# Feature projections as pairs of 64-row matmuls, with a mode-aware list schedule and a new step order

## The chip, the cores and the metric

One core of a Trainium2 chip. The metric is the device time of one execution in microseconds (us), lower is better. Most kernels here were run four times. Ratios are computed as the mean time of one kernel's runs over that of the kernel before in the same rounds, so they are not quite the ratio of the medians that are quoted.

## The reference

Linear attention with an exponential feature map, then a mixture of experts in which every token visits all eight experts. Only the first part is touched by the change.

```python
batch, n_heads, seq, head_dim, d_feat = 8, 8, 576, 64, 128
def phi(x):
    proj = np.einsum('bhsd,df->bhsf', x, w_phi)          # contraction over 64
    proj = proj - np.max(np.abs(proj), axis=-1, keepdims=True)
    return np.concatenate([np.exp(proj), np.exp(-proj)], axis=-1)
q_p, k_p = phi(q), phi(k)
kv  = np.einsum('bhsf,bhsd->bhfd', k_p, v)
num = np.einsum('bhsf,bhfd->bhsd', q_p, kv)              # den: the same with sums of k_p
# ... x = num/den; routing P by 8 Sinkhorn iterations
# out = sum over e of P[:, e] * (relu(x @ w1[e]) @ w2[e])
```

The contraction of the projection is 64 long, and TensorE has 128 rows. Two heads (a "pair") are stacked on the 128 partitions, so there are two ways to project them: one matmul against a weight that is zero in the half of the other head, or two matmuls of 64 rows each, one per head, in the two row halves of the array at once.

## The kernel before

All operations of the kernel are first put into a plan with an assumed duration and its dependences, then a list scheduler sorts them: it keeps a clock per engine and always issues the operation that can start first, ties going to the step order, a string of 322 letters. The sorted list is then the fixed program of each engine. Nothing is moved at run time. An engine that has to wait waits with everything behind it.

```python
wphi2 = a_in.tile([128, 2, DF], BF16)      # [64 rows of w_phi | 0] and [0 | 64 rows of w_phi]

def tokens(pp, stat, n, r, takes=()):      # scores of 128 tokens, both heads in one matmul
    for c in range(n):                     # n = 4
        pe(256, lambda c=c: mm(pp[1][2 * c // n]()[:, 1024 // n * c % 512:][:, 0:256],
                               stat(c), wphi2f, True, True), ...)

def feature_rows(pt, mov, r):              # query features, transposed
    for x in range(2):
        pe(512, lambda x=x: mm(pt[1][x]()[:, 0:512], wphi2[:, x, :], mov(), True, True), ...)
```

From the third batch on, q and k are loaded by a transfer that GpSimd issues, into one of two `qk` buffers. A transposing transfer issued by SyncE then turns the buffer into `qkT`, after which the buffer may be loaded again. GpSimd also computes: the negated maxima and the scaled v of every pair.

```python
def load_qk(b, hh, nh, t, r=()):           # b >= 2; "POOL" is GpSimd's queue
    for x, src in ((1, k), (0, q)):
        dma("POOL", nh << 17, 230, lambda x=x, src=src: nc.gpsimd.dma_start(out=t["qk"]()...))
def turn_qk(t):
    dma("SP", 1 << 19, 148, lambda: nc.sync.dma_start_transpose(out=t["T"]()..., in_=t["qk"]()...))
...
pool(8, lambda: nc.gpsimd.tensor_scalar_mul(m()[:, 1], m()[:, 2], -1.0), ...)     # in pair_a
exp(16, lambda: em(), lambda: m()[:, 1:3], 1.0, ...)                              # ScalarE needs it
pool(1024, lambda: nc.gpsimd.tensor_tensor(out=s["v"]()..., op=ALU.mult), ...)
```

The softmax here doesn't subtract the row's maximum and nothing guards it: scores larger than these inputs give would overflow.

## Time and profile before

| | before |
|---|---|
| median | 1026.8 us (1026.7 to 1027.5, 4 runs) |
| attention, to the last gate matmul | 0 to 205.6 us |
| the rest, same work in both kernels | 821 us |

The prediction shows the page's head, the table by stage and the groups concerned. In such a table each row is a stretch of time, and "busy" is the time in which an engine has an instruction open. A matmul's record holds a tail of 164 ns beyond its pace, so gaps shorter than that can't be seen in TensorE's busy time.

### The profile page before, as it was taken

How to read it: one execution, taken by the hardware profiler on the slowest of the kernel's cores; microseconds unless marked ns; L12 is line 12 of the kernel's file. 1: busy time of each engine (PE TensorE's matmuls, PEld its weight loads, DVE VectorE, ACT ScalarE, POOL GpSimd, SP SyncE). 2: the span in 40 equal slices, each digit the busy share in tenths (PEclk: the TensorE clock that was granted, in tenths of full speed). 3: DMA queues.
4: the chain of work that ended last, by engine and by line, in shares of the span. 5: the costliest groups of instructions: out<-in, count | busy, mean ns of one | idle time of the engine just before them, and what ended most of it. 6: DMA issues, size and time to landing. Idle time of an engine off the chain costs nothing.

```text
span 1026.8 us, 24281 instructions
## 1 busy us (share of the span) xinstructions
PE 1008.1 (98%) x9469; PEld 837.9 (82%) x9504; DVE 823.5 (80%) x1600; ACT 703.9 (69%) x1530; POOL 458.5 (45%) x480
## 2 busy tenths in 40 slices
PE   7899999999999999999999999999999999999998
PEld 4666666645888888888888888888888888888886
DVE  7999989987888887787777877787778877787775
ACT  7999999834888766666666666666665666666663
POOL 5768664400334444444444434544444433444342
PEclk9999999999999999999999999999999999999999
DMA  9999978170232611161115211341116111614333
GB/s 235 192 197 179 177 137 130 37 154 19 85 104 85 124 42 42 47 129 43 48 46 112 54 43 42 75 102 42 42 46 131 42 42 43 130 36 125 133 124 124
DMA packets 112501, 96.03 MB, mean 94 GB/s; under 512 B 54145, under 2 KB 87041, under 8 KB 112385
## 3 DMA queue, kind: packets, MB, share of 16 engines
q1 hardware_dynamic: 80576, 70.55, 26.5%
q0 software_dynamic: 31648, 23.86, 16.6%
q8 instruction: 74, 1.21, 0.5%
q14 instruction: 43, 0.34, 0.1%
q10 hardware_dynamic: 160, 0.07, 0.0%
HBM read 94.98 MB, written 14.16 MB: 106 GB/s over the span
## 4 chain that ended last, share of the span: by engine, by line
PE 93%; ACT 2%; DVE 1%; DMA 1%; SPq 1%; issue 1%; POOL 0%; DVEq 0%; ACTq 0%
PE ps L1273 74%; PE ps L573 17%; PE ps L856 2%; DMA acc<-in_q_dram 1%; ACT q L569 1%; ACT k L569 0%; SPq L495 0%; ACT wx L569 0%; SPq L551 0%; PE ps L885 0%; DMA xd<-S 0%; DVE ps L864 0%; DVE hT L1305 0%; DVE m L565 0%; POOL wx L761 0%
## 5 line engine op out<-in xcount | busy, mean ns | idle before, releaser
L1428 POOL TENSOR_TENSOR acc<-acc,V 128x512 f32<-128x512 f32 x248 | 314.8, 1280 | 484.5 <-ACT V L1425 426.7
L1301 ACT COPY U<-ps 128x512 f32<-128x512 f32 x378 | 217.0, 586 | 166.2 <-PE ps L1273 150.9
L1305 DVE CUSTOM_DVE_ANT_0 hT<-ps,U 128x512 bf16<-128x512 f32 x378 | 254.6, 687 | 87.7 <-PE ps L1273 59.9
L1425 ACT ACTIVATE V<-ps,P 128x256 f32<-128x256 f32 x496 | 208.1, 473 | 90.7 <-PE ps L1273 82.1
L1413 DVE SCALAR_TENSOR_TENSOR acc<-ps,P,acc 128x256 f32<-128x256 f32 x372 | 159.1, 478 | 69.5 <-PE ps L1273 69.2
L1273 PEld LDWEIGHTS <-S 128*128 128x128 bf16 x1984 | 194.1, 98 | 22.6 <-issue 0.2
L1273 PEld LDWEIGHTS <-T 128*128 128x128 bf16 x1512 | 148.0, 98 | 17.2
L1273 PEld LDWEIGHTS <-hT 128*128 128x128 bf16 x1488 | 145.6, 98 | 16.8
L1273 PE MATMUL ps<-X,T 128*128 128x256 bf16 x1008 | 152.4, 273 | 0.0
L1273 PE MATMUL ps<-T,S 128*128 128x256 bf16 x1056 | 135.8, 273 | 0.0
L1273 PEld LDWEIGHTS <-wx 128*128 128x128 bf16 x1152 | 112.7, 98 | 13.6 <-issue 0.2
L1181 DVE TENSOR_TENSOR S<-hT 128x1024 bf16<-128x1024 bf16 x124 | 87.2, 712 | 10.1 <-ACT hT L1310 9.9
L1273 PEld LDWEIGHTS <-w 128*128 128x128 bf16 x864 | 84.5, 98 | 9.8
L1273 PE MATMUL ps<-xT,wx 128*128 128x256 bf16 x576 | 88.4, 273 | 0.1
L1273 PE MATMUL ps<-X,wx 128*128 128x256 bf16 x576 | 86.8, 273 | 0.0
L1310 ACT ACTIVATE hT<-ps 128x512 bf16<-128x512 f32 x126 | 73.2, 606 | 9.8 <-PE ps L1273 9.8
L1273 PE MATMUL ps<-wx,hT 128*128 128x256 bf16 x560 | 77.6, 273 | 0.0
L1273 PE MATMUL ps<-xT,T 128*128 128x256 bf16 x504 | 76.7, 273 | 0.0
L573 PE MATMUL ps<-xT,w 128*128 128x512 bf16 x270 | 70.5, 379 | 0.7
L573 PE MATMUL ps<-w,hT 128*128 128x512 bf16 x276 | 69.8, 379 | 0.7 <-ACT q L569 0.2
L1273 PE MATMUL ps<-T,hT 128*128 128x256 bf16 x496 | 69.2, 273 | 0.0
L1273 PE MATMUL ps<-xT,w 128*128 128x256 bf16 x432 | 66.5, 273 | 0.0
(129 smaller groups left out, 1426.5 us busy)
## 6 DMA issues: line engine op xcount, KB each, us to landing
X<-xd SPq DMA_DIRECT2D x126, 256.0 KB, 2.7
wx<-in_moe_w_dram POOLq DMA_DIRECT2D x8, 1024.0 KB, 12.4
v_m<-in_v_dram SPq DMA_DIRECT2D x15, 512.0 KB, 5.6
out_dram<-acc SPq DMA_DIRECT2D x14, 512.0 KB, 2.9
w<-in_moe_w_dram POOLq DMA_DIRECT2D x6, 1024.0 KB, 12.1
xd<-S SPq DMA_DIRECT2D x18, 256.0 KB, 2.1
qk<-in_k_dram POOLq DMA_DIRECT2D x12, 256.0 KB, 5.5
qk<-in_q_dram POOLq DMA_DIRECT2D x12, 256.0 KB, 6.4
```

Source lines behind the costliest of these rows:

```text
L569: act(el, lambda: nc.scalar.activation(out=dst(), in_=src(), func=ACT.Exp, bias=0.0, scale=scale), r, w)
L573: nc.tensor.matmul(out_, lhsT=lhsT, rhs=rhs, start=start, stop=stop)
L856: pe(65, lambda j=j: nc.tensor.matmul(pn()[:, j * D1:j * D1 + D1], lhsT=s["T"][x]()[:, j % 2, 2 * h + j // 2, :] if j < 4 else r["T"][x]() ...
L1181: lambda: f.tensor_tensor(out=out_(), in0=x(), in1=y(), op=op), r, w, **kw)
L1273: pe(256, lambda i=i, k=k, z=z: nc.tensor.matmul(bank()[:, 256 * i:256 * i + 256], lhsT=lhs(k, i), rhs=rhs(k), start=first and z, stop=k = ...
L1301: act(512, lambda: nc.scalar.copy(out=u[fp][n]().rearrange("p a b -> p (a b)"), in_=x[fp]()), [x[fp]], [u[fp][n]])
L1305: dve(515, lambda: nc.vector._custom_dve(ADD_SAT, out=out_(fp, i, j), in0=bank[fp]().rearrange("p (a b) -> p a b", a=2), in1=u[fp][n](), s ...
L1310: act(512, lambda: nc.scalar.activation(out=out_(fp, i, j), in_=x[fp]().rearrange("p (a b) -> p a b", a=2), func=ACT.Relu, bias=0.0, scale ...
L1413: dve(320, lambda n=n, ts=ts: nc.vector.scalar_tensor_tensor(out=acc[g][:, ts, 256 * j:256 * j + 256], in0=bank()[:, 256 * n:256 * n + 256 ...
L1425: act(370, lambda n=n: nc.scalar.activation(out=u()[:, n, :], in_=bank()[:, 256 * n:256 * n + 256], func=ACT.Copy, bias=0.0, scale=P[:, 4 ...
L1428: pool(695, lambda: nc.gpsimd.tensor_tensor(out=acc[g][:, 2 * i:2 * i + 2, 256 * j:256 * j + 256], in0=acc[g][:, 2 * i:2 * i + 2, 256 * j: ...
```

## The change

Its intent: let the two heads of a pair run at once in the two row halves. A change between 128-row and 64-row matmuls costs TensorE time, so the scheduler adds 0.096 us to the start of an operation that would leave the 64-row mode, which keeps such operations together. The step order was searched anew for these costs.

```diff
-                    if t is not None and (best is None or (t, o.idx) < best[:2]):
-                        best = (t, o.idx, o)
+                    key = t
+                    if eng == "PE" and o.tiled != clock.tiled:
+                        key += 0.096 if clock.tiled else 0.0
+                    if best is None or (key, o.idx) < best[:2]:
+                        best = (key, o.idx, o, t)
 ...
+    wphi = a_in.tile([128, DF], BF16, name="wphi")
 ...
-    TI, GR, KM, QM, PM, NM, RM = 0, 0, 0, 0, 0, 0, 0
+    TI, GR, KM, QM, PM, NM, RM = 1, 0, 0, 0, 0, 0, 0
 ...
+    dve(64, lambda: nc.vector.tensor_copy(out=wphi, in_=wphi_f), ["wphi_f0", "wphi_f1"], ["wphi"])
 ...
     order = (
-        "lraeaepqbwlqaqawwabwmqlltnrbppnwqb..."
+        "leaawrqlrlwpaqatbwaqpeqqbpwanmmalw..."
```

With `TI = 1` a branch that already stood in the kernel is taken:

```python
def rows():
    for c in range(n):
        for x in range(2):
            nc.tensor.matmul(pp[1][x]()[:, 128 * c:128 * c + 128],
                             lhsT=stat(c)[64 * x:64 * x + 64],
                             rhs=wphi[64 * x:64 * x + 64], start=True, stop=True)
o = plan.op("PE", n * 0.056, 0.22, rows, r + ["wphi"], pp[0], takes)
o.tiled = 1
```

More of the change, by code (lines that the diff above doesn't have):

```diff
@@ L281, in schedule @@
                     t = self.start(o, f)
-                    if t is not None and (best is None or (t, o.idx) < best[:2]):
-                        best = (t, o.idx, o)
+                    if t is None:
+                        continue
+                    key = t
[3 more added lines that the diff above has]
+                        best = (key, o.idx, o, t)
             landed = links.next()
@@ L290, in schedule @@
             assert best is not None, "no operation can start"
-            at, _, o = best
+            o, at = best[2:]
             ready[o.eng].remove(o)
@@ L997 @@
             [f"wphi_f{i}"], ["wphi2"])
+    dve(64, lambda: nc.vector.tensor_copy(out=wphi, in_=wphi_f), ["wphi_f0", "wphi_f1"],
+        ["wphi"])
     load_qk(0, 2, 2, halves[0, 0])
@@ L1053 @@
     order = (
-        "lraeaepqbwlqaqawwabwmqlltnrbppnwqbppmrmanbqaqmwwacmpnpbccpwbtcnmqnaqbclupunm"
-        "taumquglcapalbcpnqqdcenmucugbblnapmrcqdutabnqpmunpbambccddnqplanmqmducpblttb"
-        "augnaqlnrbdcampcadmqeutunqcppmdcaqtdqabpbbmlrqtdnpmuaqualbnagnacctbmqulupran"
-        "tdpmtdqcmdnpdabdancpcabbqmpumqbcdgnappqunburqcbugmmnqdcdanumupqbnucmcpnmbddp"
-        "bqmpncncubncmmgccg"
+        "leaawrqlrlwpaqatbwaqpeqqbpwanmmalwbawtppanmbbmcwpnqwmpalnlabaqmqncccuuqlncre"
+        "tpbmpbntqtcnapmlqqpbbapccqulbapbqrmbuqpualnnuunaqdmpanpnmqmltcbmtdrmubcbcden"
+        "qpbgdmdcccatqbutmbandnllcnuracmdpgqbudnupgcaudmatpnquumqpglnaqdbactcnbmmbcpn"
+        "rqdpmqbbcanqaqacpdmapumtauunqbudducqcbpburmdgbpnnumnqpcmddmangdbdpmpqmccbndp"
+        "ncugccnaqmbpcmuncg"
     )
```

## The prediction

> **What bounds the kernel now.** I read the page's head first: busy time of each engine over the whole span.
>
> ```profile
> span 1026.8 us, 24281 instructions
> PE 1008.1 (98%) x9469; PEld 837.9 (82%) x9504; DVE 823.5 (80%) x1600; ACT 703.9 (69%) x1530; POOL 458.5 (45%) x480
> ```
>
> TensorE looks like the bound, but the change touches only the first fifth of the span (attention, 0 to about 206 us), so a table by stage came next: busy time of each engine in stretches of 25 us, then the routing stage.
>
> ```profile
> 0.00:25.00 25.00, 17.62 (x155) 12.32 (x156) 19.24 (x35) 18.64 (x46) 12.78 (x27) 1.00 1.05 235
> 25.00:50.00 25.00, 20.87 (x244) 14.66 (x244) 24.30 (x56) 24.74 (x64) 18.81 (x32) 1.00 1.26 188
> 50.00:75.00 25.00, 23.99 (x319) 16.94 (x324) 23.83 (x59) 23.70 (x57) 17.76 (x29) 1.00 1.09 198
> 75.00:100.00 25.00, 24.74 (x287) 16.68 (x289) 24.06 (x59) 23.70 (x61) 21.32 (x34) 1.00 1.23 189
> 125.00:150.00 25.00, 24.79 (x267) 15.63 (x269) 23.15 (x53) 24.56 (x65) 17.41 (x32) 1.00 0.82 148
> 175.00:200.00 25.00, 24.78 (x309) 16.50 (x311) 23.24 (x58) 23.99 (x57) 11.81 (x18) 1.00 0.26 48
> 205.00:250.00 45.00, 44.70 (x239) 20.85 (x242) 36.93 (x97) 16.93 (x30) 1.62 (x2) 1.00 0.41 88
> ```
>
> Columns: window, its length, then PE, PEld, DVE, ACT, POOL busy. Two things are to be seen. From 75 to 200 us PE has no free time (24.7 to 24.8 of 25). But ACT (23.7 to 24.7) and DVE (21 to 24) are nearly as full, and from 25 to 50 us both are fuller than PE (24.3 and 24.7 against 20.9). Attention is a stage with three almost equal bounds. After 205 us PE alone is full: expert-0 matmuls fill the time of the routing chain, then the expert products follow to the end, PE at 100 of 100 us in every window. The changed kernel has that same work after attention, so **the end moves by as much as attention's end moves**, if the routing chain stays hidden.
>
> The groups that the change touches, and the timeline for the pace of such matmuls in a run:
>
> ```profile
> L573 PE MATMUL ps<-wphi,qkT 128*128 128x256 bf16 x256 | 40.7, 275 | 1.8 <-ACT qkT L711 0.5 <-DVE m L565 0.3 <-DVE wx L565 0.2
> L573 PE MATMUL ps<-qkT,wphi 128*128 128x512 bf16 x60 | 19.5, 387 | 0.7 <-DVE wx L843 0.3 <-DVE m L565 0.3
> L573 PE MATMUL ps<-wphi,rT 128*128 128x256 bf16 x32 | 5.3, 273 | 0.6 <-ACT qr L569 0.2 <-DVE rT L634 0.2
> ```
>
> ```profile
> 121.27 0.68 PE L573 MATMUL ps<-wx 128*128 128x65 bf16 x16
> ...
> 126.86 0.59 PE L573 MATMUL ps<-qkT,wphi 128*128 128x512 bf16 x2
> ...
> 129.91 0.60 PE L573 MATMUL ps<-wphi,qkT 128*128 128x256 bf16 x4
> ```
>
> A record of 273 ns is no cost: it holds the pipe's tail. The pace is the run's length less one record, over the others: 256 columns (0.60 - 0.273)/3 = 0.109 us; 512 columns 0.59 - 0.379 = 0.21 us, and 0.216 us elsewhere in such runs; 65 columns, each with its own weight load, (0.68 - 0.194)/15 = 0.032 us. The tail is 273 - 109 = 164 ns.
>
> **What the Trainium skill says.** "TensorEngine Tiling (Array Packing)", Tiling Modes, Key Properties: tiles work in parallel, but "changing tiling mode (not just tile) drains the TensorE". The trace before has only 128*128 matmuls, so it shows no switch. "TensorE: Matmul & The Clock Gate", Step-by-step: a drain takes about 128 cycles and is normally hidden under the next matmul; the 164 ns tail beside a 109 ns pace agrees that something is hidden. The same page, The mechanism (Part 3), has matmuls on different row groups start about 4 ns apart; no 64-row pair is in this trace. "TensorEngine Tiling (Array Packing)", Performance Considerations, PSUM Bottleneck: tiling speeds TensorE but not the evacuation from PSUM. This trace agrees: ACT, which with DVE does the evacuation, has at most 1.3 us free in every 25 us window from 25 to 200 us.
>
> **Part by part.** (1) Token projections. Before, 4 matmuls of 256 columns per group against a weight that is half zeros. After, 8 matmuls of 128 columns, two at once on the row halves. Groups: 32 pairs x 2 (keys, queries) + 8 rests = 72. Before 4 x 0.109 = 0.436 us. After at best 4 pairs x 0.055 = 0.22 us; if each load and matmul still needs the 32 ns that the 65-column run shows, 8 x 0.032 = 0.26 us. Saved: 72 x 0.18 to 0.22 = 13 to 15.5 us. (2) Query features in transposed form: 32 times two 512-column matmuls, now at once: 32 x 0.216 = 6.9 us saved. Sum 20 to 22.5 us of PE time, about 21.
>
> (3) Added: mode switches. In the built instruction order of the changed kernel the 640 half-row matmuls (72 x 8 + 32 x 2) stand in 74 unbroken stretches, so 148 switches; the scheduler's preference for the current mode has joined 104 operations into these. Each exposes a drain: estimated at least 128 cycles (53 ns at 2.4 GHz, from the page) and at most the whole 164 ns tail. I take 0.1 us, close to the 0.096 us that the kernel's own scheduler assumes: 148 x 0.1 = 15 us, range 8 to 24. **Net PE gain 21 - 15 = 6 us**, between -4 and +14.
>
> (4) ACT, DVE. A key bank now holds one head's four chunks in place of two chunks of both heads: same count and size of maxima and exponentials for the pairs. The rests do 2 exponentials of 512 where they did 4 of 256: 16 ACT instructions less, some 0.05 us each, under 1 us. DVE has one small cast more. So the evacuation load is unchanged, and with it a floor: ACT is busy 189.9 of the first 205 us (the windows summed), so attention can't end more than some 15 us earlier whatever PE does.
>
> (5) Order. After the last gate matmul the same expert-0 filling remains: of its 576 matmuls, 369 stand before that point in the old order, 371 in the new. So no filling was moved in or out; the gain must come as a shorter attention stage.
>
> How much of 6 us arrives? Only 222 of the 356 affected matmul records lie in 75 to 205 us, where PE is full: 62%. There it converts well, less what ACT and DVE hold back; before 75 us PE waited anyway (25 - 20.9 = 4.1 us in the second window alone). I take about two thirds: 4 us. The step order was searched anew and could win another 1 to 2 us, above all in the first 75 us, where 7.4 + 4.1 + 1.0 = 12.5 us of PE is idle. Attention ends some 5 to 6 us earlier: **1026.7 - 5.7 = 1021.0 us**.
>
> **Rivals.** *Switching eats it all:* at the full 164 ns tail, 148 x 0.164 = 24 us exceeds the saving, and the time is 1026 to 1030. For it: no trace shows the drain. Against: the author built a schedule with the smaller cost and kept the change.
> *ACT and DVE become the bound:* PE gains even 14 us but the stage shortens by 2 or 3, because the evacuation is at 23 to 24.7 of 25 us; time about 1024. For it: the table above. Sign: PE idle in 75 to 200 us grows while ACT stays at 24 or more.
> *Everything converts:* a drain near 53 ns, a gain of 13 us on PE, and an order that closes the start's gaps; 1011 to 1014. Against: the ACT floor.
> *The routing chain shows:* its last table is written near 242.6 us and the filling ends at 250.5. Both move together, so I give this little.
>
> **Range and chances.** The switch cost spans 18 us by itself, but ACT and DVE cap the good side and the re-search of the order cushions the bad side: 1012 to 1028. Faster by over 2% needs under 1006.1, a gain of 20.5 us: the whole PE saving at free switches. Chance 0.03. Slower by over 2% would need 20 us of loss: 0.02. Within 2%: 0.95.
>
> **What would show it.** Eight token matmuls in about 0.22 to 0.26 us of pace, partners starting a few ns apart, feature pairs in about 0.22 us: step 1 and 2. Start-to-start gaps of about 0.1 us more at each change between 64-row and 128-row matmuls: step 3; over 0.16 us would make me wrong towards slower. ACT still 24 of 25 us and PE falling below 24 in 75 to 200 us: the second rival. The last gate matmul near 200 us in place of 205.8, and everything after it as long as before: step 5. If the weight loads of 64 rows do not hide, or the first operations wait longer for data in the new order, the time would be above the range.

## The result, and the profile after

The changed kernel takes **1040.6 us** (1039.4 to 1042.7, 4 runs): 1.35% slower, ratio 1.0135, interval 1.0117 to 1.0152. The prediction was 1021.0, range 1012 to 1028. Its output is correct.

The head of its page:

```profile
span 1040.9 us, 24814 instructions
PE 1010.1 (97%) x9752; PEld 828.9 (80%) x9792; DVE 824.0 (79%) x1601; ACT 703.3 (68%) x1514; POOL 458.8 (44%) x480
```

This tells nearly nothing: TensorE is 2 us busier in 14 us more. The tail of each kernel, as one stretch of 821 us, tells where not to look. First before, then after:

```profile
205.00:1026.00 821.00, 816.85 (x7272) 708.97 (x7275) 637.25 (x1175) 514.02 (x1067) 326.25 (x262) 1.00 0.30 77
```

```profile
219.00:1040.00 821.00, 817.02 (x7273) 708.96 (x7277) 637.54 (x1176) 513.62 (x1066) 326.67 (x262) 1.00 0.30 77
```

Shifted by 14 us they are the same. The last gate matmul starts at 219.9 us in place of 205.6, so the whole loss lies in attention. The table by stage of the changed kernel, to be read against the one in the prediction (window, length, PE, PEld, DVE, ACT, POOL busy, granted clock, mean busy share of the DMA engines, which can pass 1 as the tool counts it, GB/s):

```profile
25.00:50.00 25.00, 21.21 (x329) 15.48 (x330) 24.80 (x62) 24.12 (x57) 19.25 (x32) 1.00 1.10 205
50.00:75.00 25.00, 23.76 (x323) 14.42 (x325) 23.55 (x59) 24.64 (x60) 19.11 (x31) 1.00 0.95 158
75.00:100.00 25.00, 19.81 (x231) 11.30 (x234) 18.17 (x39) 18.40 (x44) 18.32 (x29) 0.90 1.31 194
...
125.00:150.00 25.00, 18.11 (x240) 10.83 (x244) 16.46 (x40) 17.38 (x43) 13.66 (x24) 0.92 1.21 153
...
175.00:200.00 25.00, 24.39 (x343) 14.83 (x345) 22.58 (x54) 24.73 (x62) 14.49 (x23) 1.00 0.42 93
```

Two windows stand out, 75 to 100 and 125 to 150 us. In them *all* engines have dropped together, TensorE by 4.9 and 6.7 us, ScalarE by 5.3 and 7.2 against the kernel before. If one engine had become the bound, it would have stayed full. When all empty at once, they wait for one another, or for something that is none of them. The granted clock dips to 0.90 and 0.92 there as well. This agrees with the Trainium skill, "TensorE: Matmul & The Clock Gate", Part 1, by which the clock is halved after an idle window of about 3.4 us: TensorE idled up to 6.0 us, and in the 4 us after that stall (147 to 151 us) the granted clock is 0.50.

The list of waits names the one that everything else waits for (engine, line, waited for: us in total, times, longest). Before, GpSimd's q/k loads had only this entry of any size:

```profile
POOL qk L501 <- issue: 1.5, 5, 0.3
```

After:

```profile
POOL qk L507 <- DMA qkT<-qk: 13.9, 4, 6.9
...
ACT wx L575 <- POOL wx L765: 7.2, 2, 6.9
...
PE ps L601 <- ACT wx L575: 6.0, 1, 6.0
```

One stall, on GpSimd's timeline (start, us, engine, line, operation; what ended the idle time before it in brackets):

```profile
137.44 0.28 POOL L773 CAST v<-em 128x16 bf16<-128x16 f32 x1
144.61 0.81 POOL L507 DMA_DIRECT2D qk<-in_k_dram  x1 [6.89 <-DMA qkT<-qk]
145.41 0.76 POOL L507 DMA_DIRECT2D qk<-in_q_dram  x1
146.17 0.27 POOL L765 TENSOR_SCALAR wx<-wx 128x8 f32<-128x8 f32 x1
```

and on the chain that ended last, in order of time:

```profile
134.79 9.26 DMA qkT<-qk
...
144.61 0.54 POOL qk L507
...
146.17 0.28 POOL wx L765
...
146.60 0.58 ACT wx L575
...
148.30 0.61 PE ps L619 x2
```

GpSimd is to issue a load into a `qk` buffer. The transposing transfer that still reads the buffer lands only at 144.05 us, 9.3 us after its issue. For 6.9 us GpSimd stands still, and the instruction behind the loads, a 0.27 us negation of maxima that has nothing to do with the buffer, stands with it. ScalarE's next instruction needs that negation and waits 6.86 us; TensorE's next scores need the bank that ScalarE is to empty, and wait 6.02 us. **A load that was ordered too early has stopped the kernel.**

The issue-to-landing times of these transposes (min, median, max), before and after:

```profile
DMA to landing us min/median/max: 4.3/5.9/8.2
```

```profile
DMA to landing us min/median/max: 4.5/6.8/11.0
```

The scheduler's own constants give 4.6 us for one that is alone (1.6 us to start, 512 KB at 265 GB/s, 1.0 us to be seen), and more while GpSimd's queue also moves data. It places the next load for the moment the buffer should come free. Its plan can be compared with the trace, transpose by transpose (how the plan was had stands at the end of the experiments). Before, none of the twelve lands more than 1.5 us slower after its issue than planned. After, eight land 1.2 to 4.7 us slower than planned. The one of this stall is the worst: 4.6 us planned, 9.3 us in the trace.

What of TensorE itself? A piece of its timeline after:

```profile
205.49 0.28 PE L862 MATMUL ps<-wx 128*128 128x65 bf16 x4
205.60 0.20 PE L862 MATMUL ps<-wx,qr 128*128 128x65 bf16 x1
205.73 0.39 PE L619 MATMUL ps<-qkT,wphi 64*128 64x512 bf16 x2
205.96 0.39 PE L601 MATMUL ps<-wphi,qkT 64*128 64x128 bf16 x8
206.28 0.29 PE L579 MATMUL ps<-vrd,kr 128*128 128x130 bf16 x2
```

A 65-column matmul paces at 0.032 us, but the first half-row one starts 0.13 us after it: 0.10 us for the switch. The two 512-column halves need 0.23 us together, where two full-row ones need 0.43. The eight 128-column halves take 0.32 us to the next full-row matmul: 0.22 of pace and 0.10 of switch. Over all records of the trace, start to start after a full-row 512-column matmul is 312 ns (median of 40) into the other mode and 216 ns within its own. On the way back, it is 149 ns from the last half-row 128-column matmul (median of 50), where pairs of them pace at 56 ns. So a switch costs **about 0.095 us, 148 times** (the trace has 148), and partners start 3 to 4 ns apart. This side came out as predicted.

### The profile page after: what moved, and what is told of

Its sections match the earlier page's. It is cut to its first block, busy times and chain, and to the rows that moved or that the text cites. A ratio compares the mean times of both kernels' runs of the same rounds, so it can differ in the third digit from the quotient of the medians.

```text
span 1040.9 us, 24814 instructions
## 1 busy us (share of the span) xinstructions
PE 1010.1 (97%) x9752; PEld 828.9 (80%) x9792; DVE 824.0 (79%) x1601; ACT 703.3 (68%) x1514; POOL 458.8 (44%) x480
## 4 chain that ended last, share of the span: by engine, by line
PE 85%; ACT 4%; DMA 4%; DVE 2%; POOL 2%; issue 1%; SPq 0%; POOLq 0%; ACTq 0%; DVEq 0%
PE ps L1281 73%; PE ps L579 10%; DMA qkT<-qk 3%; ACT wx L575 1%; PE ps L862 1%; ACT k L575 1%; ACT q L575 1%; PE ps L601 1%; POOL qk L507 1%; DMA acc<-in_q_dram 1%; POOL v L767 1%; DVE m L571 1%; PE ps L619 0%; POOL vrd L689 0%; ACT hT L940 0%
## 5 line engine op out<-in xcount | busy, mean ns | idle before, releaser
L1281 PEld LDWEIGHTS <-S 128*128 128x128 bf16 x1984 | 194.1, 98 | 22.7 <-issue 0.2
L1281 PEld LDWEIGHTS <-T 128*128 128x128 bf16 x1512 | 147.9, 98 | 17.4 <-issue 0.2
L1281 PEld LDWEIGHTS <-wx 128*128 128x128 bf16 x1152 | 112.7, 98 | 13.6 <-issue 0.2
L1189 DVE TENSOR_TENSOR S<-hT 128x1024 bf16<-128x1024 bf16 x124 | 87.2, 712 | 10.1 <-ACT hT L1318 9.9
L579 PE MATMUL ps<-w,hT 128*128 128x512 bf16 x271 | 73.1, 386 | 1.3 <-issue 0.7
```

Of the source, the lines that this page charges most:

```text
L579: nc.tensor.matmul(out_, lhsT=lhsT, rhs=rhs, start=start, stop=stop)
L1189: lambda: f.tensor_tensor(out=out_(), in0=x(), in1=y(), op=op), r, w, **kw)
L1281: pe(256, lambda i=i, k=k, z=z: nc.tensor.matmul(bank()[:, 256 * i:256 * i + 256], lhsT=lhs(k, i), rhs=rhs(k), start=first and z, stop=k = ...
```

## The experiments

The first theory (A): the loss is the new order's stalls at GpSimd, and the half rows gain a little. Rivals: the half rows themselves cost the time (B); the transfers are simply late, so whatever needs their data waits however the loads stand (C). Two attempts could not be built: the new order with full rows planned as before, and the old order with half rows but without the preference. In both the scheduler came to a point where no operation could start. Orders, costs and buffer counts hang together.

**1. The old step order with half rows and preference** (the order string of before in the changed kernel).

> The half-row matmuls and the scheduler's preference as in the changed kernel, but with the step order of the kernel before. Theory A (the loss of 14 us is the new step order: GpSimd stands twice in front of a q/k load whose buffer a transposing transfer still reads, and the GpSimd work behind it starves ScalarE, VectorE and TensorE; the half rows themselves gain a few us): 1018 to 1027 us, no GpSimd wait for such a transfer over 1 us. Theory B (the half rows cost the time themselves, by mode switches or by what they do to PSUM or the clock): 1035 us or more.

Measured: 1043.4 us (1039.6 to 1045.5), ratio 1.0153. A miss for theory A as stated, and a number inside theory B's range. But the trace holds the cause that theory A names:

```profile
POOL qk L507 <- DMA qkT<-qk: 7.8, 2, 5.9
...
ACT em L575 <- POOL m L765: 5.4, 2, 5.0
PE ps L601 <- ACT q L575: 4.7, 1, 4.7
```

The same kind of stall, near 90 us. So it isn't *the new order*; with other assumed costs the scheduler makes another plan of the old order too, and that plan stalls in the same way. Theory B is left to experiment 2.

**2. The changed kernel's schedule with full-row matmuls.** Every engine keeps its program; only the halves are replaced.

```diff
-                                     lhsT=stat(c)[64 * x:64 * x + 64],
-                                     rhs=wphi[64 * x:64 * x + 64], start=True, stop=True)
+                                     lhsT=stat(c), rhs=wphi2[:, x, :],
+                                     start=True, stop=True)
 ... and in feature_rows:
-                nc.tensor.matmul(..., lhsT=wphi[half], rhs=mov()[half], ...)
+                nc.tensor.matmul(..., lhsT=wphi2[:, x, :], rhs=mov(), ...)
```

> The changed kernel's schedule on every engine, instruction by instruction, but each half-row matmul issued as a full-row one against the half-zero weight, so no mode switch and no halves. Theory A: the two GpSimd stalls of 3 to 7 us stay, and TensorE has some 6 us more work: 1040 to 1048 us. Theory B: the loss goes away with the halves: 1026 to 1034 us.

Measured: 1042.9 us (1042.0 to 1044.7), ratio 1.0162. The stalls stand as before:

```profile
POOL qk L507 <- DMA qkT<-qk: 13.3, 4, 6.8
```

As theory A said, the loss stays without any half row, and theory B falls. In this schedule the half rows are worth some 2.3 us (1042.9 - 1040.6, from different rounds; the two intervals overlap, so this is not clear of the noise).

**3. One pair of loads moved.** After sorting, the two loads that blocked GpSimd for 6.9 us are moved behind the next four GpSimd instructions. They could not issue before the buffer was free anyway. No other instruction changes its place.

```diff
         done = self.schedule()
+        later = {21: 4, 20: 4}                   # which q/k load, past how many GpSimd operations
 ...
+            done.insert(j, done.pop(i))          # the cut part finds i and j, never past its reader
```

> The changed kernel with the one pair of q/k loads that blocked GpSimd for 6.9 us moved behind the next four GpSimd instructions; every other instruction in its place. Theory A: the stall near 140 us and its clock dip go, 6 to 9 us less than the changed kernel: 1031 to 1035 us. Theory C (the transfers themselves are late, and whatever needs q and k waits anyway): 1038 to 1042 us.

Measured: 1035.9 us (1034.9 to 1036.6), ratio 1.0091: 4.7 us less for the place of two instructions. That is 0.9 us above theory A's range and 2.1 us below theory C's: the direction of A, with a smaller gain than the 6 to 9 us expected. GpSimd's timeline there:

```profile
137.39 0.24 POOL L777 TENSOR_SCALAR wx<-wx 128x8 f32<-128x8 f32 x1
...
139.57 1.91 POOL L779 TENSOR_TENSOR wx<-v_m,wx 128x1024 bf16<-128x1024 f32 x1 [1.81 <-ACT wx L587]
141.55 0.26 POOL L785 CAST wx<-wx 128x16 bf16<-128x16 f32 x1
144.30 0.83 POOL L519 DMA_DIRECT2D qk<-in_k_dram  x1 [2.50 <-DMA qkT<-qk]
```

The load issues at 144.3 us as before (144.6), so the transfer is exactly as late. But the negation runs at 137.4 and not at 146.2, and TensorE is busy 23.3 us of this window where it was 18.1:

```profile
125.00:150.00 25.00, 23.31 (x346) 14.54 (x345) 22.35 (x54) 21.92 (x54) 15.55 (x26) 1.00 1.35 153
```

Theory C falls for this stall: the transfer was late in both, and what stood behind the load made the loss.

**4. Three pairs of loads moved** (also those that blocked for 2.8 and 3.5 us near 80 us).

> As the run before, and also the two pairs of loads that blocked GpSimd for 2.8 and 3.5 us near 80 us moved behind 5 and 2 GpSimd instructions. Theory A: both stalls go: 1023 to 1031 us. Theory C: 1038 to 1042 us.

Measured: 1035.9 us (1032.4 to 1037.0), ratio 1.0086. A miss: nothing gained in the median over experiment 3. The window 75 to 100 us did recover in its trace, which is of its fastest run, 1032.4 us (TensorE 22.7 us), but the next load blocked GpSimd for 3.4 us at 102 us. Mending by hand moves the stall to the next load.

**5. A margin in the scheduler.** A `qk` buffer (or one of the remainder rows, `qk_r`) counts as free some us later than the modelled landing of its transpose, for the reuse of the buffer alone. The loads that reuse it then stand later in GpSimd's program. The rest of the plan changes with them.

```diff
                 if b.left == 0:
-                    b.ring.give(b.end, b.slot)
+                    b.ring.give(b.end + (4 if o.turn and o.unit == 30 and "qk" in b.ring.tag
+                                         else 0.0), b.slot)
```

> The changed kernel (half rows, new order) with one change in the list scheduler: a q/k buffer counts as free 4 us later than the scheduler thinks its transposing transfer lands, so the load that reuses it stands later in GpSimd's order. Theory A (every stall is GpSimd standing in front of a load whose buffer is freed later than planned): GpSimd's waits for such transfers fall under 2 us in sum, 1018 to 1029 us. Theory B (half rows cost the time themselves): no better than 1033 us.

Measured: **1031.3 us** (1028.5 to 1033.4), ratio 1.0040: 9.3 us less than the changed kernel, though above the range. Its waits and its two windows:

```profile
POOL qk L507 <- DMA qkT<-qk: 1.1, 1, 1.1
```

```profile
75.00:100.00 25.00, 23.96 (x320) 13.33 (x318) 23.59 (x58) 22.09 (x52) 17.40 (x29) 1.00 1.28 199
...
125.00:150.00 25.00, 24.30 (x330) 14.32 (x330) 23.34 (x56) 25.00 (x60) 16.46 (x24) 1.00 1.03 172
```

The transposes of this run are no quicker (median 6.6 us, longest 10.7). The stalls are all but gone, and the clock is whole in these windows. (The trace is of the fastest of the four runs, 1028.5 us.)

**6. The same schedule with full rows**, edited as in experiment 2.

> The schedule of the run before on every engine, with full-row matmuls in place of the pairs of half rows. Gives the worth of the half rows alone where stalls are few. If a mode switch costs 0.1 us as the changed kernel's timeline suggests, TensorE has about 6 us more work here and the time is 3 to 7 us above the run before. If the half rows are worth nothing or cost: equal or below.

Measured: 1034.3 us (1033.6 to 1036.0), ratio 1.0077, in the same rounds as experiment 5. So the half rows are worth 3.0 us here, at the low end of what was expected. Some 0.9 us of it, and of the 2.3 us in experiment 2, is an artefact: the stand-in's 576 full-row matmuls of 128 columns pace at 56 ns, where the kernel before pays 109 ns for 256 columns, 54.5 for as many.

**7 and 8. The kernel before, planned anew.** Full rows, old order; only an assumed cost of the scheduler is changed by a trifle: 0.5 ns per matmul, or 2 ns per ScalarE operation.

```diff
-        plan.op("PE", max(cols / 2400.0 + 0.0025, 0.031), 0.22, fn, r, w, takes)
+        plan.op("PE", max(cols / 2400.0 + 0.0030, 0.031), 0.22, fn, r, w, takes)
```

> The kernel before, full rows, old order; only the scheduler's assumed cost of a matmul is 0.5 ns higher, so that it plans anew. Theory D (the plan of before was picked by its time on the chip, and any new plan meets some GpSimd stalls): 1030 to 1042 us. Theory E (full-row plans are robust, and plans made for half rows are tighter, so only these stall): 1025 to 1029 us.

> As the run before, with ScalarE's assumed fixed cost 2 ns higher in place of it. Theory D: 1030 to 1042 us. Theory E: 1025 to 1029 us.

Measured: 1029.2 us (ratio 1.0021, interval 1.0006 to 1.0036) and 1030.8 us (1.0040, 1.0025 to 1.0055). The first lies between the two theories and the second in theory D's range: a new plan of the old kernel costs 2.2 and 3.8 us. But GpSimd's longest wait for a transpose is 1.0 us in the second and none shows in the first, so the stalls that theory D has for a reason are not there. No other plan seen matched the one of the kernel before. Whether that plan had been picked by its time on the chip can't be told from here.

**9 to 14. More margins.** New order with 2, 3, 5 and 6 us; old order with 4 and 6 us.

> As the 4 us margin with the new order, but 2 us. Theory A predicts something between the changed kernel (1040.6) and the 4 us margin (1031.3): 1031 to 1038 us, with a wait of GpSimd for a transposing transfer still visible.

> Half rows, new order, 3 us margin. Between 1031 and 1037 us if the stalls shrink smoothly with the margin (2 us gave 1036.8, 4 us 1031.3); a value outside says that the plan a margin happens to give weighs as much as the margin.

> Half rows, new order, 5 us margin: between 1031 and 1036 us if smooth (6 us gave 1036.0); under 1026.5 us it would be a version that beats both kernels.

> As the 4 us margin with the new order, but 6 us. If late landings still cost, a longer margin helps: 1024 to 1030 us; if 4 us already covers them and a later load starves the next pairs: 1030 to 1036 us.

> Half rows and preference with the old step order (1043.4 us without a margin) and the 4 us margin. Theory A: the stall near 90 us goes, 1024 to 1034 us. If the old order's loss had another cause: 1038 us or more.

> As the run before with 6 us in place of 4. 1022 to 1034 us by theory A; a version under 1026 us would beat both kernels and show the half rows' gain in the total.

| margin, us | 0 | 2 | 3 | 4 | 5 | 6 |
|---|---|---|---|---|---|---|
| new order, us | 1040.6 | 1036.8 | 1031.5 | 1031.3 | 1032.0 | 1036.0 |
| old order, us | 1043.4 | | | 1034.7 | | 1033.3 |

The new order's four values lie in their ranges (6 us at the upper end of the second case, 1030 to 1036). So does the old order's 6 us; its 4 us missed the range of 1024 to 1034 by 0.7 us. All seven plans with a margin beat the same order without one, by 3.8 to 10.1 us. GpSimd's waits for `qkT<-qk` in the new order are 13.9, 5.0, 5.1, 1.1, 2.0 us at margins 0, 2, 3, 4, 5. They aren't all: 2 and 3 us have the same waits and times 5.3 us apart. At 6 us there is none left, and TensorE now waits 4.2 us for a transpose of the remainder rows (`rT<-qk_r`), which needs such a load: too late is a cost as well. No version beat the kernel before.

**15 and 16. The preference**, at the 4 us margin: taken out, and doubled to 0.2 us. In the built instruction order these have 182 and 132 switches, against 146.

> Half rows, new order, 4 us margin (1031.3 us so far, 146 switches), without the scheduler's preference for the current row mode: 182 switches in the built order, 36 more, each 0.095 us by the timeline, so 3.4 us more TensorE time; 1032 to 1036 us. If the choice of plan weighs more than the switches, it may lie anywhere between 1027 and 1037 us.

> The same with the preference doubled to 0.2 us: 132 switches, 14 fewer, 1.3 us less TensorE time: 1028 to 1031 us if switches decide, anywhere between 1025 and 1037 us if the plan does.

Measured: 1054.1 us (1049.8 to 1054.6) and 1046.7 us (1045.3 to 1048.9). Both miss every estimate by the number of switches: 36 more would be 3.4 us and it lost 22.8; 14 fewer should gain 1.3 us and it lost 15.3. They are other plans, and neither trace has a GpSimd wait for `qkT<-qk`. With the doubled preference another transposing transfer sits on the chain that ended last, `xT`, which the margin doesn't cover:

```profile
122.98 11.79 DMA xT<-wx
```

Without the preference VectorE and ScalarE are half empty for one window, TensorE's clock falls to 0.80, and the chain that ended last runs there through short steps of TensorE, VectorE and ScalarE in turn, with no transfer in it:

```profile
100.00:125.00 25.00, 19.25 (x171) 9.78 (x170) 13.43 (x32) 12.33 (x28) 7.60 (x14) 0.80 0.48 74
```

**What the plans themselves say**. The scheduler is plain Python and can be run without the chip. With stubs in place of the tile and engine calls, `schedule()` of the kernels gives 148, 146, 182 and 132 switches for the changed kernel and experiments 5, 15 and 16, as counted above, and a time at which its plan ends. That time is the scheduler's assumption and no measurement; "measured" are the medians from above.

| us | before | exp. 7 | exp. 8 | changed | exp. 1 | exp. 5 | old order, 4 us | exp. 15 | exp. 16 |
|---|---|---|---|---|---|---|---|---|---|
| end of the plan | 1022.9 | 1028.2 | 1027.1 | 1020.4 | 1030.1 | 1024.6 | 1030.7 | 1040.0 | 1032.9 |
| measured | 1026.8 | 1029.2 | 1030.8 | 1040.6 | 1043.4 | 1031.3 | 1034.7 | 1054.1 | 1046.7 |
| over the plan | 3.9 | 1.0 | 3.7 | 20.2 | 13.3 | 6.7 | 4.0 | 14.1 | 13.8 |

The plan of the changed kernel promised 2.5 us less than the plan before, and it was missed by 20 us where the other was missed by 4. With the margin the miss falls to 6.7 and 4.0 us. In experiments 15 and 16 much of the loss stands in the plan already: 15.4 of 22.8 us and 8.3 of 15.3 us. The hole of experiment 15 is there too: in its plan VectorE works 14.2 and ScalarE 13.7 us between 100 and 125 us. And the plan before is the shortest of the three full-row plans, so it may have been picked without the chip.

## Why the prediction was wrong

By its own steps:

- **What bounds the kernel, and that the end moves with attention's end:** right. The two 821 us tails agree; attention's end moved by 14.3 us in the traces and the time by 13.7.
- **Part (1) and (2), the saving:** right. Pairs of halves start 3 to 4 ns apart, 0.22 us for eight of 128 columns, 0.23 us for two of 512.
- **Part (3), 148 switches at 0.1 us:** right. 0.095 us each, 14.1 us in all. An estimate from the measured paces puts the net on TensorE at some 8 us (72 x 0.212 + 32 x 0.207 - 14.1), near the 6 of the prediction.
- **Part (4), the unchanged work of ScalarE and VectorE:** right. Busy 703.9 and 823.5 us before, 703.3 and 824.0 after.
- **"How much of 6 us arrives?", two thirds or 4 us:** too high. In one and the same schedule the half rows were worth 2.3 and 3.0 us, 1.4 and 2.1 without the stand-in's longer form. The second rival may be at work here in the small (ScalarE and VectorE are nearly full, so time that TensorE saves becomes gaps), but no run shows that alone.
- **The step that failed: the order.** Part (5) found no filling moved and took the rest of the new plan to be as sound as the old, and the sum then gave it a gain: "The step order was searched anew and could win another 1 to 2 us". The range leaned on it too ("the re-search of the order cushions the bad side"). The new plan lost 16.4 us (1042.9 with full rows against 1026.4 in the same rounds). I had compared how many filling matmuls stand before attention's end. I had not compared where the q/k loads stand in GpSimd's program, nor asked what stands behind them. Some 9 us of the loss go when the reloads are ordered 4 us later: with full rows in both, the distance to the kernel before falls from 16.4 to 7.2 us (1034.3 against 1027.1 in the same rounds). Of these 7.2, 0.9 are the stand-in's longer form, and 2 to 4 is what a trifling new plan of the old kernel cost as well. The rest I can't put down to one cause. It is the plan and not the order string: the old string, planned with the new costs, lost as much (experiment 1).
- **The rivals:** none named this. I looked for a new bound at TensorE, ScalarE, VectorE and in the routing chain, not at GpSimd, which is 45% busy over the span. In attention it is busier, and the prediction's own table showed it: 21.3 of 25 us in the window 75 to 100. My last sentence did name first operations that wait longer for data, but that is the start of the kernel, and the stalls are at 75 to 100 and 125 to 150 us.
- **The sign I gave for the second rival** (TensorE falls while ScalarE stays at 24 us) did its work: ScalarE fell too, to 18.4 and 17.4, which ruled that rival out as the main cause at first sight.

That a late landing plus the in-order GpSimd makes the stall is shown, by experiment 3 for the longest one; experiment 5 and the other margins agree, though each of them is a new plan as a whole. That these transposes land later than planned in the changed kernel is shown by plan and trace. A long landing alone does no harm where the plan allows for it: in experiment 8 one took 13.6 us (12.3 planned), and GpSimd's longest wait for a transpose was 1.0 us. Why they land later than planned in one kernel and not in another was not tested. The order of events fits transfers that crowd each other (DMA share 1.31 in the window 75 to 100), but the kernel before has 1.23 in that window and no stall.

## What to carry to other kernels

A change that makes a static scheduler plan anew is two changes, and the new plan can cost more than the operation saves: run the new plan with the old operation, and the old kernel with a trifling new plan, before giving the operation credit or blame. Compare the end of the plan with the time on the chip as well: it tells a long plan from a plan that is not kept. On an engine that both computes and issues loads, look at what stands *behind* each load in its program; a load ordered a few us too early stops everything after it, while in experiment 3 the same load, ordered later, issued no later than before. When all engines of a window empty together, look for an in-order queue that waits for a buffer, on an engine that nobody thinks of as the bound, or for a chain of short steps from engine to engine (experiment 15).

## What the Trainium skill lacked or had wrong

- "TensorEngine Tiling (Array Packing)", Key Properties, says that a change of the tiling mode drains TensorE, and gives no figure. Here each change costs about 95 ns in both directions (start to start: 312 against 216 ns after a full-row 512-column matmul, 149 against 56 ns after a half-row one of 128).
- "TensorE: Matmul & The Clock Gate", Back-to-back issue gap, gives a sustained pace of about 81 ns at 128 columns and 131 ns at 512 for pairs of weight load and matmul, and says that the formula of the isolated gap is off. In these runs, each matmul with its own weight load, the pace is 56 ns (full rows, experiments 2 and 6) and 216 ns, as that formula has it.
- "DMA: Bandwidth & Descriptors", Latency and other measured facts, gives 261 GB/s for a transposing transfer, which would be 2 us for 512 KB (an estimate from the page's figure). It has no figure for issue to landing beside other traffic; here that is 4.2 to 13.6 us, median 5.9 to 8.4 by kernel.
- "DMA: Bandwidth & Descriptors", Anatomy of one DMA, puts a transfer's semaphore wait on the engine that issues it, but neither it nor another page that I read draws the consequence: a load issued by GpSimd which waits for its buffer holds up GpSimd's computing instructions behind it. Here the longest such wait was 6.9 us, and it reached TensorE as 6.0 us.
